# A new written-out order for a two-branch kernel, and D's second copies made with a maximum

## The chip, the core and the metric

The kernel runs on one core of one Trainium2 chip. Its time is the device time of one execution in microseconds (us); of the kernel before three runs gave a median of 131.97 us (131.25 to 135.03). Of one execution there is a profile, and all trace times below are microseconds from the start of its span. The engines are called PE (matrix multiply), DVE (vector), ACT (scalar), POOL (GpSimd) and SP (here only the queue that issues nearly all transfers).

## The reference

Two independent branches over 2048 tokens of 448 channels, in bf16, are joined along the channels.

```python
# branch A: attention of 16 heads of 28 over 8 earlier tokens, 2 apart
idx = pos[:, None] - 2 * arange(8)[None, :]           # masked where negative
logits = einsum("bhsd,bhswd->bhsw", q, k[idx]) * 28 ** -0.5
a = einsum("bhsw,bhswd->bhsd", softmax(logits), v[idx]) @ wo
# branch B: a diagonal complex state-space model of 448 states
h_t = Lam_bar * h_{t-1} + B_bar @ x_t                 # Lam_bar = exp(dt * Lam)
b = 2 * (h @ C^T).real + x * Dskip
out = concatenate([a, b], axis=-1)
```

## The kernel before

**Steps and the order.** Every small piece of work is a Python function marked as a step (`@op`). One long string, `ORDER`, lists all 700 steps with their arguments; the kernel emits them in that sequence. A number behind `@` gives the PSUM bank or the buffer slot that a step takes, and a trailing `.` or `=` says whether ACT or DVE does an eviction or a scaling. Each engine runs its own instructions strictly in the sequence of the string, and semaphores hold an instruction until what it needs is there. So the string fixes the order on all engines, the order of the transfers on SP's queue, the banks and the buffers at once.

**Branch A.** `XI`, `XA`, `XH` and `xi`, `xa`, `xh` bring the input into transposed form (`xT`) by PE and evictions for the first half, `TX` by DMA transposes for the second. `QS` and `QT` compute a 512-token piece of q or k (three matmuls over full rows, one over the last 64 rows), `qk` and `qh` evict it. `VM`, `VT`, `v` do the same for v. `P(u, r, ws)` on DVE (L387) multiplies q with four shifted k at once; there are 28 of them, 14 for each half `u` of the tokens, in seven buffer slots of `prt`. `E_` sums the products of a head on PE, `lt` on ACT scales the logits of one half, `TD` turns them by a DMA transpose (L417). `sma` (DVE: mask, maximum, subtract), `smb` (ACT: Exp), `smc` (DVE: sum, reciprocal, multiply) are the softmax of one half. `AL`, `al`, `ad`, `sp` build banded matrices of the weights through DRAM, in buffers that `pm`, `pk` and `pw` clear on POOL, `AV` multiplies them with v, and `W_` applies `wo`.

**Branch B.** Time is cut into four phases `j` of 512 steps, states into seven groups `g` of 64 complex ones. `LB` loads x, four DMA transposes `xt` (L720) turn it into `xbuf`, of 14 blocks of 128x128 each, and one, `BD` (L678), turns the input matrix into `BT`, 28 blocks. `BU` and `BH` (L736, L743) project x on a group; each reads 512 columns to which all four `xt` contribute. `BR` adds the rotated earlier phase, `z` evicts, `UP`, `y`, `sa`, `sb`, `sd`, `DN`, `dn` run the scan over the last phase. `sw`, `hp`, `hy`, `hz` then carry the scan's state back into the other phases: `hp` makes scaled copies in numbered buffers, `hy` adds two of them (L864), and the last step of a group, `hz` (L869), adds the result into `Z`. `C(j, ct)` (L883) is an output group of seven matmuls, one for each `g`; for `j` under 3 it reads `Z` after `hz`, for `j` of 3 it does not. `CH` (L907) is one such group in two halves. `c` and `ch` evict with D's share of x added, `oc` and `oh` store. `CS` copies the transposed C matrix, and `ca`, `cb`, `cs` scale it.

**D.** `LD` loads the vector Dskip, broadcast to 128 partitions, as columns 0 to 447 of the tile `dsk`. `dk` (L729, L730) makes a second copy of it in columns 448 to 895, in two parts, and `xd` multiplies x by the tile.

Of the kernel before, what the change touches and what calls it, by code (L numbers as in the profile page):

```python
# [29 lines left out]


ORDER = """
LR LX24 LX02 WU@0 LH0 LQ10 XI1@0 xi11. xi10= LQ11 LH1 LQ00 LX48 LQ01 PP@1 pcopy pa XI2@2 xi20= LY1 LY2 LY0 LV LB111
LB001 LB121 LB011 LB000 TX3 TX2 TX0 XI0@3 TX1 pb pd_ xi00. pe QT030@2 QT020@1 pc xi01. ty0@0 tf0 LB021 QT040@0
QS020 ty5@1 tf5 WX qk020. QS030 qk030. pf QS050@3 QS040 ts00 qk040. LB101 QS060@2 QS000@1 P021@0 P020@1 XH1@4 xh1=
XA11@5 xa11. XA10@6 xa10. QS010@7 QT001@5 pg QT000 QT021@4 QT050 QT010 qk050. QT051@0 P041@2 P040@3 QT060 qh000.
qh001. QT011@6 qk000. qk010. P000@4 ts05 LC QS021 QS061@3 P001@5 QS001 QS011 QS051 ts10 ts15 qk001. qk011. P011@6
qk051. ts25 qk021. VM110@7 QS031@1 VM100@6 ts20 VT110 QT061 ty2@1 tf2 QT031 qk031. VT100 v100. qh010. E_00@0 E_02
E_04 P030@2 VM101@4 xt3 qh011. VM001@6 v110. ts02 QS041@1 LN1 P010@3 VT101 v101. LB110 QT110@7 QT041 QT130@3
QT111@5 QT120@2 VT001 P031@0 qk041. P051@1 QS111 ts12 hc0 LN0 P060@5 ts22 qk111. ty1@1 tf1 v001. QS101@1 ty6@0  # L40
QS130 QS110 QS120 qk120. qk110. ts01 QS141@6 QS100@5 ci3. CD3 VM400@2 P050@4 E_01@7 E_03 E_05 qk130. ci2. CD2
QT151@3 VT400 QT100 qk100. tf6 ts06 P061@3 ts11 QT141 QT150@4 QT101 qk101. ts21 E_06 lt01 v400. qk141. QS150
VM511@5 QS151 QS131@1 LB120 qk151. P121@1 P101@5 P120@3 lt00 QS121@2 VT500@6 qk150. QT131 LB100 xt1 TD0 LB020
qk131. ty3@1 QT140@3 VT511 P110@4 QT160@7 QT121 qk121. VM500 QS140 v500. P100@0 v511. QS161@1 xt2 bx= QS160 qh100.
qh101. hc1 P151@2 E_10@6 E_12 P111@6 E_11@5 LB010 BD VT510@7 QT161 ts16 VT000@2 qk140. P131@0 P130@6 VM011@4 qh110.
xt0 VM000 v000. P141@4 VM510 v510. P150@1 VM501@3 VM410@2 VM411@7 ts26 qh111. VM010@1 ci1. P140@3 VT410 ty4@0 LD
CD1 VT501 v501. VT010 v010. P160@5 VT011 v011. ci0. E_13 E_15 E_14 VM401@1 P161@0 E_16 v410. VM111@4 lt10 ab lt11
VT411 BH32@6 VT401 sma0 smb0 v401. BH10@2 CD0 VT111 OZ TD1 rb0 tf4 BH00@5 BU10 BU00 v111. z00. v411. BU20@3 BU01@0
OP pw BU30@1 z10. wo BH30 BH01 dk smc0@0 CS BH51@5 BH20 z20. BH11@4 BH40@7 BR01 z01. z30. BU40 z40. sma1 BU11 BR11
rb3 z11. AL0@1 al0. AL1@7 al1. tf3 smb1 BU31@4 smc1@0 BH13@1 ca1= ca3= ts03 BH02@7 BH23@0 BH12@3 BH31 BH03@2 cb3=  # L50
xd0 BU02 BR02 z02. BR31 BU12 BR12 z12. BU13 BU03 BR03 cb4. z31. pm01 pm12 pm02 BR13 z03. z13. cb0. BU32 BR32 UP0
pm13 ts13 cb6= UP1 pm03 AX@4 z32. y1. AL2@3 pm11 pk pm21 pm10 AL3@7 pm00 pm22 y0. sa0 ca0= BU21@6 sb0 ca6= ad1 ax.
BH50@2 cb5= BH41@4 BH33@1 al2. ts04 BH22@3 ca2. BH21 BR21 BU33 BU22 ts14 ad0 z21. BR33 BR22 sp1 al3. ts24 z22. BU50
BU23 BR23 sd0 cb2= cb1= ca5. BU41 BR41 z33. ad2 ts23 DN1@3 dn1 z23. z50. UP3 y3= pm20 pm23 adx sp0 UP2 DN0@7 dn0
z41. y2. cs0 sa2 hp001@3. hp021. BU60@2 BU51 BR51 BH42@7 ca4= hp000@2. BH52@0 hp020. BH60 ad3 BH43@1 spx BH63@4
BH53@3 hp010. z51. BU42 z60. BR42 z42. BU52 AV010@5 AV000@6 sw0 sb2 av000. BR52 BU43 z52. cs2 BR43 hp011. av010.
BU53 BR53 z53. sd2 DN2@0 z43. DN3@6 cs4 dn2 AV031@7 av031. dn3 cs6 AV001@5 UP5 y5. hp101@4= UP4 hp100@0= hp110= y4.
sa4 AV030@0 av030. hp003@1. sp2 hp121= AV011@7 AV020@3 av020. AV021@6 sp3 BH62@1 BH61@0 BU61 BR61 av021. z61. BU62
W_00@6 BR62 BU63 sb4 av011. av001. W_31@5 hp120= z62. BR63 hp013. W_11@1 sd4 hp023. hy0 z63. hp002@6. UP6 DN5@7 dn5
y6. sa6 w31@0. sw2 hp012. hp022. W_30@0 DN4@4 dn4 sw4 w30@1. w11@2. w00@3. hp005@0. hp025. W_21@7 ow00 w21@4.  # L60
W_10@5 W_20@4 w20@5. hp015. sb6 W_01@1 hp111= sd6 C32@6 ow21 hz0 hy1 DN6@7 dn6 AV110@0 ow20 AV100@4 AV131@3 AV120@2
av110. AV130@7 hz1 ow30 hp103@7= hp102@5= AV101@0 hp123= av100. hp113= av120. hp112= hy3 hp105@3= hp122= av130.
hp104@2= hp114= hp125= AV111@4 av101. hz3 AV121@2 av121. av111. w10@3. av131. sw6 hy2 w01@5. hp004@7. hp124= W_60@7
w60@1. hp024. hp014. hz2 hy4 hp115. hy5 hp106@3= W_70@0 ow60 ow31 hp116. ow01 hz4 W_50@4 w50@1. W_41@5 hp006@2.
W_40@1 W_61@7 w61@5. ow11 hp126= hz5 w40@2. ow40 hp026. W_71@3 C30@2 C31@4 W_51@7 C33@1 hp016. hy6 hz6 w71@2= xd2
w70@0. w41@4. ow70 C10@0 c10@0 xd3 c30@1 oc30 xd1 c31@2 C02@5 C22@3 ow41 ow10 C13@0 c13@3 oc13 c33@1 oc33 c22@4
oc31 ow50 C03@2 c03@5 w51@3= c02@3 oc03 oc22 ow71 oc02 ow61 C11@4 C12@1 c11@1 ow51 C01@2 c01@2 oc01 oc11 c12@5 oc12
C21@4 c21@4 c32@3 C20@2 c20@6 oc32 oc21 C00@4 oc20 oc10 c00@1 CH0@2 ch0@5 CH1@6 oc00 ch1 oh0 oh1
"""

@with_exitstack
def kernel(
# [653 lines left out]

    @op
    def dk():
        V.tensor_copy(dsk[:, 512:896], dsk[:, 0:384])  # L729
        V.tensor_copy(dsk[:, D:512], dsk[:, 384:D])  # L730
# [273 lines left out]
```

## Time and profile before

| | before |
|---|---|
| median of three runs | 131.97 us |
| the profiled execution's own time | 131.99 us |
| its span in the trace | 130.3 us |
| PE busy | 119.8 us (92%) |
| DVE busy | 115.3 us (88%) |
| ACT busy | 99.3 us (76%) |
| POOL busy | 21.5 us (17%) |
| mean granted PE clock | 0.987 |
| moved by DMA | 23.02 MB, mean 177 GB/s |

Busy shares are means over the whole span: ACT has nothing to do in the last 18 us, when PE works through the output groups and DVE evicts them. A busy PE is one that has matmuls in its pipeline, at whatever clock. The idle time in front of an instruction is put down to what released it last.

### The profile page before, as it was taken

To read this page: it belongs to the slowest core of one execution; us is meant where nothing else is said; L and a number is where in the kernel's file an instruction comes from. 1 tells how busy PE (TensorE), PEld (TensorE's weight loads), DVE (VectorE), ACT (ScalarE), POOL (GpSimd) and SP (SyncE) were. 2 spreads that over 40 slices of the span, in tenths; PEclk is the share of its full clock that TensorE was granted. 3 is DMA by queue.
4 is the path that set the end of the run, shared out by engine and by line. 5 is a ranking of instruction groups with operands and counts; after the bars stand their busy time and mean duration, and the time that the engine had idled before them with its cause. 6 is when DMAs were issued, how large, how long until landed. Compare 5 with 4: busy or idle time off the path is not lost.

```text
span 130.3 us, 2886 instructions
## 1 busy us (share of the span) xinstructions
PE 119.8 (92%) x1046; PEld 57.8 (44%) x1046; DVE 115.3 (88%) x229; ACT 99.3 (76%) x204; POOL 21.5 (17%) x50
## 2 busy tenths in 40 slices
PE   6969999999999992899999999999999959999990
PEld 6525343343443430235354444555566424455560
DVE  5788999999999998499499999999999995999871
ACT  3479999999999999348999999999999949100000
POOL 6811300000000000699980000000000000000000
PEclk9999999999999999679999999999999999999999
DMA  3999998899999999996599895799863031115673
GB/s 96 265 245 301 310 149 172 248 247 205 119 276 223 185 211 149 198 240 166 225 264 122 268 167 190 142 135 144 142 171 101 34 107 35 35 35 166 226 240 113
DMA packets 55317, 23.02 MB, mean 177 GB/s; under 512 B 41127, under 2 KB 54503, under 8 KB 55303
## 3 DMA queue, kind: packets, MB, share of 16 engines
q1 hardware_dynamic: 55240, 22.84, 82.4%
q8 instruction: 8, 0.13, 0.5%
q14 instruction: 6, 0.05, 0.2%
q10 hardware_dynamic: 63, 0.01, 0.0%
HBM read 9.74 MB, written 6.37 MB: 124 GB/s over the span
## 4 chain that ended last, share of the span: by engine, by line
PE 43%; DVE 34%; DMA 8%; issue 6%; ACT 3%; SPq 2%; ACTq 1%; DVEq 0%
PE ps L883 13%; PE ps L351 13%; DVE pr L387 5%; DMA wq<-in_A_wqkv_dram 4%; PE ps L736 4%; DMA xbuf<-xnB 4%; DVE hs L791 3%; PE ps L515 3%; DVE p L777 2%; DVE p L776 2%; PE ps L357 2%; PE ps L399 2%; DVE Z L869 2%; ACT Z L125 2%; DVE Ak L864 2%
## 5 line engine op out<-in xcount | busy, mean ns | idle before, releaser
L387 DVE TENSOR_TENSOR pr<-qf,kf 128x2048 bf16<-128x2048 bf16 x24 | 27.8, 1219 | 0.7 <-ACT kf L125 0.6
L736 PE MATMUL ps<-xbuf,BT 128*128 128x512 bf16 x84 | 22.9, 404 | 0.0
L883 PE MATMUL ps<-Cw,Z 128*128 128x448 bf16 x105 | 20.7, 352 | 1.6 <-ACT ya L125 1.6
L351 PE MATMUL ps<-xT,wq 128*128 128x512 bf16 x84 | 19.8, 380 | 1.2 <-DMA wq<-in_A_wqkv_dram 1.2
L125 ACT CAST Z<-ps 128x512 bf16<-128x512 f32 (+1 forms) x34 | 15.9, 525 | 3.5 <-issue 2.2
L883 PEld LDWEIGHTS <-Z 128*128 128x128 bf16 x105 | 10.2, 98 | 11.6 <-issue 1.9
L553 PE MATMUL ps<-wo,oT 128*128 128x448 bf16 x64 | 13.3, 352 | 0.0
L736 PEld LDWEIGHTS <-BT 128*128 128x128 bf16 x84 | 8.2, 103 | 10.8 <-issue 3.8
L351 PEld LDWEIGHTS <-wq 128*128 128x128 bf16 x84 | 7.8, 98 | 11.8 <-DMA wq<-in_A_wqkv_dram 2.2
L948 POOL MEMSET PT<- 128x1080 f32 x12 | 11.5, 1006 | 0.0
L515 PE MATMUL ps<-wq,xT 128*128 128x448 bf16 x48 | 10.7, 353 | 0.0
L125 ACT CAST oT<-ps 128x512 bf16<-128x512 f32 x17 | 9.6, 651 | 0.2
L125 ACT CAST v_s<-ps 128x448 bf16<-128x448 f32 x16 | 8.3, 549 | 1.0 <-PE ps L522 0.8
L553 PEld LDWEIGHTS <-oT 128*128 128x128 bf16 x64 | 6.2, 98 | 5.8 <-issue 0.2
L857 ACT ACTIVATE Ak<-Z,acol 128x512 bf16<-128x512 bf16 x12 | 8.3, 744 | 0.0
L125 ACT CAST ya<-ps 128x448 bf16<-128x448 f32 (+1 forms) x15 | 8.0, 577 | 0.0
L743 PE MATMUL ps<-xbuf,BT 64*128 64x512 bf16 x28 | 5.1, 378 | 3.0 <-DMA xbuf<-xnB 3.0
L125 ACT CAST kf<-ps 128x512 bf16<-128x512 f32 x12 | 6.9, 603 | 0.8 <-PE ps L351 0.8
L750 PE MATMUL ps<-Z,R 128*128 128x512 bf16 x21 | 7.5, 381 | 0.0
L125 ACT CAST qf<-ps 128x512 bf16<-128x512 f32 x12 | 7.1, 593 | 0.4 <-PE ps L351 0.2
L515 PEld LDWEIGHTS <-xT 128*128 128x128 bf16 x48 | 4.3, 98 | 5.8 <-issue 2.2
L933 POOL MEMSET Z<- 128x14 bf16 x1 | 0.1, 112 | 38.6 <-PE ps L522 38.6
(177 smaller groups left out, 220.4 us busy)
## 6 DMA issues: line engine op xcount, KB each, us to landing
PT<-pd SPq DMA_DIRECT2D x16, 156.0 KB, 5.0
out_dram<-ya SPq DMA_DIRECT2D x16, 112.0 KB, 1.8
out_dram<-xbuf SPq DMA_DIRECT2D x15, 112.0 KB, 1.8
pd<-Ak SPq DMA_DIRECT2D x2, 640.0 KB, 4.1
xbuf<-in_A_x_dram SPq DMA_DIRECT2D x2, 448.0 KB, 6.1
xnB<-in_B_x_dram SPq DMA_DIRECT2D x4, 224.0 KB, 4.8
oT<-Cw SPq DMA_DIRECT2D x2, 392.0 KB, 4.9
xnB<-in_B_x_dram SPq DMA_DIRECT2D x4, 192.0 KB, 2.9
```

The costliest lines, as they stand in the source:

```text
L125: (ACT.copy if e == "A" else V.tensor_copy)(o, i)
L351: PE.matmul(p[:], wqk(m, slice(0, 128), kt), xT[:, u, 4 * s + kt], start=(first and kt == 0), stop=(not first and kt == 2))
L387: V.tensor_tensor(t, q.unsqueeze(1).to_broadcast((128, 4, 512)), k4, ALU.mult)
L515: PE.matmul(p[:, 0:D], xT[:, b0 // 4, 4 * s + kt, c + par:c + 256:2], wq[:, kt, 2 * D:3 * D], start=(first and kt == 0), stop=(not first a ...
L553: PE.matmul(p[:, 0:D], late["oT"][:, b // 4, hg, par, 128 * (b % 4):128 * (b % 4) + 128], late["wo"][:, hg, :], start=(hg == 0), stop=(hg ...
L736: PE.matmul(p[:], BT[:, g, f, :], xTB[:, j // 2, 4 * (j % 2) + f, :], start=(first and f == 0), stop=(not first and f == 2 and j == 0))
L743: PE.matmul(p[:], BT[r, g, 3, :], xTB[r, j // 2, 3, :], start=first, stop=(not first and j == 0))
L750: PE.matmul(pp["z", g, j][:], rot(g, 0), late["Z"][:, g, j - 1, :], start=False, stop=True)
L791: V.tensor_tensor_scan(hs[:, i], rk[:, 4, g0 + i:g0 + i + 1].to_broadcast((128, N2)), vv[:, i], 0.0, ALU.mult, ALU.add)
L857: ACT.activation(t, i, ACTF.Copy, scale=c)
L883: PE.matmul(p[:, 0:D], z, Cw[:, g, :], start=(g == 0), stop=(g == G - 1))
L948: POOL.memset(t.bitcast(F32), 0.0)
```

## The change

The string `ORDER` is written anew: the same 700 steps in another sequence, with other banks and buffer slots, and 18 evictions or scalings on the other of ACT and DVE. Apart from the string, `dk` makes its two copies as the maximum of the source with itself. All later lines move down by one.

```diff
 ORDER = """
-LR LX24 LX02 WU@0 LH0 LQ10 XI1@0 xi11. xi10= LQ11 LH1 LQ00 LX48 LQ01 PP@1 pcopy pa XI2@2 xi20= LY1 LY2 LY0 LV LB111
+LR LX24 LX02 WU@0 XI1@0 xi10. xi11= PP@1 pcopy pa pb pd_ XI2@2 XI0@3 xi01= LQ00 xi00. QS000@0 LX48 pe LQ01 LQ11 LH0
...
     @op
     def dk():
-        V.tensor_copy(dsk[:, 512:896], dsk[:, 0:384])
-        V.tensor_copy(dsk[:, D:512], dsk[:, 384:D])
+        for a, b, n in ((512, 0, 384), (D, 384, 64)):
+            V.tensor_tensor(dsk[:, a:a + n], dsk[:, b:b + n], dsk[:, b:b + n], ALU.max)
```

On SP's queue this is the piece around the DMA transposes, first as it stood. `xbuf<-xnB` is an `xt`, `attn<-lt` a `TD`, `BT<-Bn` is `BD`, `Cw<-Cn` turns the C matrix, and `xnB` and `Bn` from a DRAM tensor are loads.

```order
L683 DMA_TRANSPOSE Cw<-Cn 128x7x128
L252 DMA xnB<-in_B_x_dram 128x2x384
L252 DMA xnB<-in_B_x_dram 128x2x448
L720 DMA_TRANSPOSE xbuf<-xnB 128x14x128
L417 DMA_TRANSPOSE attn<-lt 128x8x128
L252 DMA xnB<-in_B_x_dram 128x2x384
L720 DMA_TRANSPOSE xbuf<-xnB 128x14x128
L252 DMA xnB<-in_B_x_dram 128x2x64
L678 DMA_TRANSPOSE BT<-Bn 128x28x128
L720 DMA_TRANSPOSE xbuf<-xnB 128x14x128
L725 DMA dsk<-in_B_Dskip_dram 128x448
L683 DMA_TRANSPOSE Cw<-Cn 128x7x128 x2
```

One `xt` stands still earlier on the queue, between the loads of C and of B. The same piece in the new order:

```order
L253 DMA xnB<-in_B_x_dram 128x2x64
L253 DMA xnB<-in_B_x_dram 128x2x384
L418 DMA_TRANSPOSE attn<-lt 128x8x128
L679 DMA_TRANSPOSE BT<-Bn 128x28x128
L721 DMA_TRANSPOSE xbuf<-xnB 128x14x128 x4
L726 DMA dsk<-in_B_Dskip_dram 128x448
L684 DMA_TRANSPOSE Cw<-Cn 128x7x128
L684 DMA_TRANSPOSE Cw<-Cn 128x7x64
L684 DMA_TRANSPOSE Cw<-Cn 128x7x128
L418 DMA_TRANSPOSE attn<-lt 128x8x128
```

All twelve loads of x now stand ahead; the first `TD`, `BD` and the four `xt` follow one another, and D's load comes behind them.

On DVE this is the piece around the first softmax, as it stood. `pr` are the products `P`, the rows with `attn` and `m` are `sma`, those with `zc` are `smc`, `R` is a rotation table, `kM` and `frt` are a step `tf`.

```order
L387 TENSOR_TENSOR pr<-qf,kf 128x2048 x7
L387 TENSOR_TENSOR pr<-qh_t,kh 128x2048 x2
L423 TENSOR_TENSOR attn<-attn,mk 128x256
L425 TENSOR_TENSOR m<-attn 128x512
L426 TENSOR_TENSOR m<-m 128x8x32
L427 TENSOR_TENSOR m<-m 128x8x16
L429 TENSOR_TENSOR attn<-attn,m 128x1024
L672 TENSOR_TENSOR R<-Is,co 128x7x128
L655 TENSOR_SCALAR kM<-iot,fT 128x256
L656 SCALAR_TENSOR_TENSOR frt<-kM,frt 128x256
L729 COPY dsk<-dsk 128x384
L730 COPY dsk<-dsk 128x64
```

And in the new order, from the end of `sma` on:

```order
L430 TENSOR_TENSOR attn<-attn,m 128x1024
L388 TENSOR_TENSOR pr<-qf,kf 128x2048 x5
L388 TENSOR_TENSOR pr<-qh_t,kh 128x2048 x2
L440 TENSOR_TENSOR zc<-attn 128x512
L441 TENSOR_TENSOR zc<-zc 128x8x32
L442 TENSOR_TENSOR zc<-zc 128x8x16
L443 RECIPROCAL zc<-zc 128x8x16
L444 TENSOR_TENSOR attn<-attn,zc 128x1024
L731 TENSOR_TENSOR dsk<-dsk 128x384
L731 TENSOR_TENSOR dsk<-dsk 128x64
L673 TENSOR_TENSOR R<-Is,co 128x7x128
L656 TENSOR_SCALAR kM<-iot,fT 128x256
```

Seven products moved from ahead of `sma` to behind it, where ACT's Exp of the first half runs, and `dk` moved behind `smc`.

More of the change, by code (lines that the diff above doesn't have):

```diff
@@ L32 @@
 ORDER = """
-LR LX24 LX02 WU@0 LH0 LQ10 XI1@0 xi11. xi10= LQ11 LH1 LQ00 LX48 LQ01 PP@1 pcopy pa XI2@2 xi20= LY1 LY2 LY0 LV LB111
[L34 to L67, printed above, removed]
@@ L68 @@
-C21@4 c21@4 c32@3 C20@2 c20@6 oc32 oc21 C00@4 oc20 oc10 c00@1 CH0@2 ch0@5 CH1@6 oc00 ch1 oh0 oh1
+LR LX24 LX02 WU@0 XI1@0 xi10. xi11= PP@1 pcopy pa pb pd_ XI2@2 XI0@3 xi01= LQ00 xi00. QS000@0 LX48 pe LQ01 LQ11 LH0
+pc XH1@3 XA10@1 LH1 ty0@0 LQ10 tf0 QS010@4 LY0 LY2 LY1 LN1 LV TX1 TX2 TX3 TX0 xh1= xi20= XA11@3 QS050@2 QS030@5 pf
+ty5@1 tf5 xa10. xa11. pg LC QT000 qk000. QT050 LN0 QT001@3 QT010 qk010. P000@0 QT031@1 QT020@6 QT011@7 ts05 QT030
+qk030. QS020 qk020. ts15 P001@1 P020@2 QS011 P021@3 ts00 LB111 ts10 QS001 qk001. ts20 WX QS060@6 QS031 LB100
@@ new lines @@
+QS021@5 qk050. VT100@3 QT051@4 QT021 QT060 qk011. P011@4 LB120 P010@5 LB011 ty2@0 tf2 qk031. LB121 LB001 QT040@2
+QT041@0 qk021. qh000. QS041 P030@6 QS051 qk051. LB000 LB020 LB110 ts25 ty1@1 tf1 qh001. QS040 qk041. VM100 ts02
+v100. VM001@4 VM101@5 QS061@1 ts01 E_01@6 E_00@0 qk040. E_02 QT061 qh010. VT001 QT150@2 QT110@3 ts12 QT111@7 LB101
+LB010 LB021 qh011. ts22 QS111 qk111. ts11 QS110 v001. qk110. QS150 QS101@1 QS140@7 QS120@4 ts21 P050@5 P031@3 hc0
+qk150. QT101 QT140 P051@2 ci2. qk101. VT111@3 bx. P040@1 E_03 E_05 P041@0 E_04 QT121@2 QT120 P060@4 ty6@1 qk120.
@@ new lines @@
+P061@3 VT101 QT130@1 E_06 lt00 tf6 QS130 P110@3 lt01 TD0 BD qk130. xt1 xt2 xt0 xt3 QS121 QS131@6 QS100@1 P111@4
+VT510@0 QT160@4 P120@0 ci3. QT131 qk140. P140@1 v101. qk121. QT141@7 QT100 qk100. LD VM111 ts06 QS160 qh100. QS141
+VM510 VM400@1 QS161@2 QS151@5 v111. qh101. VM110@4 VT110 QT151 QT161 hc1 ty3@0 VT400 v510. qk131. P100@2 ci1.
+P121@5 P101@6 E_10@6 E_12 E_11@0 sma0 qk141. qk151. P150@5 CD2 P151@4 ts16 v110. VT500@5 VT511@7 v400. qh111.
+VT410@3 VT501@4 ts26 qh110. CD3 VM511 v511. VM410 VM000@1 v410. VM011@2 VM501 v501. smb0 VM010@3 VM401@7 CD1
@@ new lines @@
+VM411@4 VM500 v500. P141@3 VT000 VT411 VT010 v000. P130@0 P131@6 E_13 E_14 E_15 ty4@1 VT401 VT011 BH00@1 P161@2
+v010. v401. P160@0 E_16 lt11 smc0@0 BU00 BH20@7 BH30@0 BH11@3 lt10 ci0. TD1 OZ CD0 OP ab BH10@5 dk v011. BH01@6
+BU20 pm22 pm01 rb0 z20. v411. BU10 z10. BU30 z30. AL0@4 al0. ad0 tf4 AL1@5 al1. z00. BU11 BR11 z11. BU01 BR01 z01.
+BU12@1 sma1 smb1 BH03@3 BH32@6 BH21@5 BH22@4 BH31@0 BH12 BH02@7 rb3 BH13@2 BU31 BU02 tf3 ts03 BR02 z02. smc1@0 BR31
+CS ca4= xd0 ca2= BR12 z12. BU03 BR03 ts13 z31. z03. ts04 BU13 BR13 z13. ca0. BU32 BR32 UP0 y0. UP1 y1. ca6= sa0
@@ new lines @@
+AX@0 ad1 ax. cb1= sb0 ca1= sd0 cb4= BU21 BR21 AL3@2 BU22 ts14 z21. cb6. pm03 z32. ca5. cb5= pw BU23@5 pm10 pm00
+pm02 sp0 adx ca3= BR22 BU33@6 BH40@0 pk BH33 BH23 BH41@3 z22. al3. pm12 pm21 pm23 cb3. ts24 BH42@4 pm13 pm11 BH50@1
+sp1 BH51@2 pm20 AL2@7 al2. BR23 cb2= ad3 BR33 wo ad2 z23. z33. BU40 z40. ts23 BU50 cb0= z50. UP3 DN0@7 UP2 y2. dn0
+DN1@0 dn1 hp000@3. BU41 BR41 cs2 cs6 cs0 y3. sa2 BU51 BR51 z41. hp020. z51. cs4 sb2 hp001@2= BU42 AV010@3 av010.
+sd2 AV000@6 av000. AV001@5 av001. sw0 AV021@0 AV030@2 AV031@1 AV020@3 AV011@7 sp3 spx sp2 BH52@6 BU52 BR42 av011.
@@ new lines @@
+BR52 av031. av021. hp101@1= hp111= hp121= hp100@0= z42. z52. BH43@1 BH61@7 BH53@0 BH60@5 hp011. av020. BU43 BR43
+z43. BU53 hp021. BR53 DN2@3 dn2 DN3@6 dn3 sw2 hp120= hy1 z53. UP4 y4. BU60 UP5 av030. y5. sa4 BH63@3 BH62@1 z60.
+hp002@4. hp012. hp110= W_00@6 w00@0. BU61 BR61 z61. sb4 hp010. hy0 BU62 W_01@5 w01@1. BR62 sd4 z62. hz1 W_20@7
+hp003@5. W_31@6 BU63 hp022. w31@2. BR63 z63. W_30@1 DN5@6 w20@3. DN4@5 ow01 dn5 hp023. UP6 y6. dn4 ow31 sw4 sa6
+AV121@0 AV130@7 AV111@2 hp102@6= sb6 hp122= sd6 AV100@6 hp112= av121. AV101@3 av111. AV120@5 W_21@0 AV110@2
@@ new lines @@
+hp103@7= av101. av120. hp113= hy2 av100. av110. av130. hp123= ow00 AV131@5 av131. hp013. hp004@9. w21@0. W_10@3
+W_70@2 hp024. W_51@7 W_11@5 w30@2. hp104@8= hp124= hy3 hp114= ow30 DN6@6 dn6 sw6 w51@1. ow20 W_40@4 w40@4. hp014.
+hp005@7. ow51 hz2 hp006@6. W_60@0 W_61@7 hp015. w61@2. w10@5. ow10 W_71@6 W_41@4 hp025. w71@3. hz0 hy4 hp105@4=
+hp115= hp125= C30@1 C33@7 hz4 C31@6 hp026. hp016. w70@5. hy5 ow71 C32@3 W_50@2 hp106@9= hp116. ow21 hz5 hz3 hp126.
+hy6 hz6 w41@0. ow41 w60@3. C00@4 C21@0 ow60 c00@0 xd2 w50@3= ow50 oc00 ow61 c30@1 ow70 oc30 xd3 c32@2 c33@3 oc33
@@ L69 @@
+C13@4 CH0@2 xd1 w11@5= c21@1 oc21 c13@3 C11@1 c11@0 C22@3 c22@4 c31@5 oc32 oc11 ow40 ow11 C12@7 c12@2 oc12 oc13
+oc22 oc31 C02@0 c02@1 ch0@0 oc02 C03@1 c03@6 C01@6 c01@7 oc01 oh0 C10@2 c10@4 C20@6 c20@7 oc03 oc10 oc20 CH1@2 ch1
+oh1
 """
```

## The prediction

> **What bounds the kernel now.** I read the page first, then the waits, then the timelines of PE, DVE, ACT and of SP's DMA queue.
>
> ```profile
> span 130.3 us, 2886 instructions
> PE 119.8 (92%) x1046; PEld 57.8 (44%) x1046; DVE 115.3 (88%) x229; ACT 99.3 (76%) x204; POOL 21.5 (17%) x50
> PEclk9999999999999999679999999999999999999999
> ```
>
> PE and DVE are both nearly full, so a new order can only win the few waits that are left, and can lose anywhere. The list of waits names them (total, times, longest):
>
> ```profile
> PE ps L743 <- DMA xbuf<-xnB: 3.0, 1, 3.0
> DVE dsk L729 <- DMA dsk<-in_B_Dskip_dram: 2.1, 1, 2.1
> DVE zc L439 <- ACT attn L433: 1.8, 1, 1.8
> PE ps L883 <- ACT ya L125: 1.6, 1, 1.6
> DVE Ak L864 <- ACT Ak L857: 1.5, 1, 1.5
> ```
>
> On PE's timeline (start, duration) the first of them costs more than its 3.0 us:
>
> ```profile
> 8.73 3.41 PE L351 MATMUL ps<-xT,wq 128*128 128x512 bf16 x15 [0.52 <-DMA wq<-in_A_wqkv_dram]
> 49.20 0.36 PE L522 MATMUL ps<-wq,xT 64*128 64x448 bf16 x1
> 52.53 0.37 PE L743 MATMUL ps<-xbuf,BT 64*128 64x512 bf16 x1 [2.97 <-DMA xbuf<-xnB]
> 53.27 5.10 PE L736 MATMUL ps<-xbuf,BT 128*128 128x512 bf16 x15
> 107.67 1.48 PE L883 MATMUL ps<-Cw,Z 128*128 128x448 bf16 x7 [1.63 <-ACT ya L125]
> 109.75 16.23 PE L883 MATMUL ps<-Cw,Z 128*128 128x448 bf16 x84
> 125.81 1.50 PE L907 MATMUL ps<-Cw,Z 128*128 128x224 bf16 x14
> ```
>
> Behind the wait 15 matmuls of 512 columns take 5.10 us where 15 like them took 3.41: the clock was down (the 6 and 7 of the page's row), another 1.7 us. PE's removable loss is 2.97 + 1.7 + 1.63 = 6.3 us.
>
> DVE decides the end. Every output group C(j, ct) with j under 3 reads all of Z, which is complete with the last `hz` (L869), and 12 groups' worth (11 of `C`, two halves in `CH`) stand behind it.
>
> ```profile
> 12.67 0.43 DVE L125 COPY xT<-ps 64x512 bf16<-64x512 bf16 x1
> 30.49 1.22 DVE L387 TENSOR_TENSOR pr<-qh_t,kh 128x2048 bf16<-128x2048 bf16 x1
> 53.78 0.55 DVE L729 COPY dsk<-dsk 128x384 bf16<-128x384 bf16 x1 [2.12 <-DMA dsk<-in_B_Dskip_dram]
> 54.25 1.05 DVE L730 COPY dsk<-dsk 128x64 bf16<-128x64 bf16 x1
> 54.33 0.97 DVE L439 TENSOR_TENSOR zc<-attn 128x512 f32<-128x512 bf16 x1
> 63.54 0.69 DVE L439 TENSOR_TENSOR zc<-attn 128x512 f32<-128x512 bf16 x1 [1.81 <-ACT attn L433]
> 110.36 0.96 DVE L864 TENSOR_TENSOR Ak<-Ak,BT 128x1536 bf16<-128x1536 bf16 x1 [1.53 <-ACT Ak L857]
> 111.36 0.96 DVE L869 TENSOR_TENSOR Z<-Z,Ak 128x1536 bf16<-128x1536 bf16 x1
> ```
>
> The last `hz` ends at 111.36 + 0.96 = 112.32, and the span runs 130.3 - 112.32 = 17.98 us longer. DVE's own removable loss ahead of it is 2.12 + 1.81 + 1.53 = 5.46 us.
>
> **The change, part by part.** *Work.* The instructions of a step stay what they were but for `dk`. Eighteen evictions or scalings change between ACT and DVE; of those ahead of the last `hz`, seven come to DVE and seven leave it, none over 0.5 us, so DVE's sum there moves by about nothing, bounds -0.5 and +0.5. PE's work is the same.
>
> *dk.* The two copies hold DVE from 53.78, and the instruction behind them ends at 54.33 + 0.97 = 55.30 where its twin takes 0.69: without `dk` it would have ended at 54.47, so the pair costs 0.83. For two-input operations of 384 and 64 columns the nearest rows are the 512 and 128 columns of the softmax's maximum:
>
> ```profile
> 58.27 0.42 DVE L425 TENSOR_TENSOR m<-attn 128x512 bf16<-128x512 bf16 x1
> 59.05 0.22 DVE L427 TENSOR_TENSOR m<-m 128x128 bf16<-128x128 bf16 x1
> 53.38 0.84 POOL L948 MEMSET wo<- 128x896 f32 x1
> 54.16 5.84 POOL L948 MEMSET PT<- 128x1080 f32 x6
> ```
>
> They are pipelined, so about 0.4 for both: a gain of 0.4, bounds 0 and 0.8. POOL's memsets ran beside both copies, and they will run beside the maxima. A rule speaks against the edit: the Trainium skill ("VectorE: DVE Perf Modes", "The perf-mode tier table") gives a bf16 copy four elements a cycle and `tensor_tensor` two. By it and that page's 58 cycles at 0.96 GHz an estimate is 0.24 us for the copies and 0.35 for the maxima: a loss of 0.1, and a total 0.5 above mine; the 0.55 and 1.05 of the trace do not agree with the 0.24.
>
> *Transposes on SP's queue, and what starts them.* SP's rows (start, time to issue):
>
> ```profile
> 14.37 6.33 SPq L256 DMA_TRANSPOSE xT<-xbuf  x4
> 38.07 1.26 SPq L417 DMA_TRANSPOSE attn<-lt  x1
> 42.99 4.19 SPq L678 DMA_TRANSPOSE BT<-Bn  x1
> 47.27 1.61 SPq L720 DMA_TRANSPOSE xbuf<-xnB  x1
> 48.93 1.19 SPq L725 DMA_DIRECT2D dsk<-in_B_Dskip_dram  x1
> 52.83 1.44 SPq L417 DMA_TRANSPOSE attn<-lt  x1
> ```
>
> Before, three of the four `xt` stand early, between loads, and the last behind `BD`; every `BU` needs all four. Now all loads come first, then TD0, BD and four `xt` in one row: 8 + 28 + 56 = 92 blocks of 128x128. The row starts when TD0's wait ends: after E_06, which needs P061. P061 is the 14th product in both orders and ended at 31.71; one `tf` (0.87) less and one small copy (0.3) more stand ahead, so 31.1. E_06 and the two `lt` behind it take 0.6 + 0.5 + 0.5, so TD0 issues at about 32.9 instead of 38.07. Price of a block: the last `xt` alone is 1.61/14 = 0.115, BD 4.19/28 = 0.15, and BD with the `xt` behind it, from 42.99 to their user's start at 52.53, 9.54/42 = 0.23 with start and landing in it; the four `xT` were issued at 6.33/28 = 0.23. I take 0.15 a block and, from 47.27 + 1.61 to 52.53, 3.6 us of landing and stalls once: 32.9 + 13.8 + 3.6 = 50.3. Bounds 47.1 (0.115) and 54.1 (0.23, landing included).
>
> *PE.* It was through with all work ahead of the first `BH` at 49.20 + 0.36 = 49.56. The same work stands ahead now. New is that E_06 comes when P061 is only just done: PE reaches it about 0.7 us early and waits. So PE asks for `xbuf` at about 50.3, as it lands: a wait near 0, bounds 0 and 3.8. Both the 2.97 and the clock's 1.7 go.
>
> *D and the second softmax.* The rows for these are from DVE, from ACT and from ACT's waits:
>
> ```profile
> 37.50 8.11 DVE L387 TENSOR_TENSOR pr<-qf,kf 128x2048 bf16<-128x2048 bf16 x7
> 62.43 1.08 ACT L433 ACTIVATE attn<-attn 128x1024 bf16<-128x1024 bf16 x1
> 108.98 1.35 ACT L857 ACTIVATE Ak<-Z,acol 128x512 bf16<-128x512 bf16 x2
> ACT Z L125 <- issue: 2.2, 1, 2.2
> ACT BT L857 <- DVE Ak L864: 1.6, 1, 1.6
> ACT Z L125 <- PE ps L743: 1.4, 1, 1.4
> ```
>
> DVE runs on from P061's 31.1: a `tf` (0.87), fourteen products of 1.14 (8.11 for seven, overlapped) and `sma0` (2.0) bring `smc0` to 49.9, and its 3.7 bring `dk` to 53.6. D's load follows the row of transposes at 46.7 and lands by 51.5 if it again takes up to the 53.78 - 48.93 = 4.85 it took: the 2.12 goes, and comes back if the row is over 2 us late. Five small steps (5.4) then bring `smc1` to 59.4. `smb1`, the Exp that it needs, waits on ACT for `z01`; PE comes there some 6 us after 50.3, Exp ends at about 56.8 + 0.5 + 1.08 = 58.4. The 1.81 goes, margin 1.0.
>
> *The last `hp`.* ACT's `hp116` waited for a buffer that DVE's `hy5` had to free (the 1.6), and `hy6` then for ACT, done at 108.98 + 1.35 = 110.33. The buffers are dealt anew (slots 8 and 9 are new), so I take that 1.6 off with the 2.2 and 1.4 of the starved middle: 105.1. DVE comes to `hy6` at 106.5 - 1.9 = 104.6 by the sum below: the 1.53 goes, and about 0.6 comes back, bounds 0 and 1.5.
>
> *Sum.* Last `hz`: 112.32 - 5.46 - 0.4 = 106.5. PE reaches its first dependent group at 109.75 + 1.32 (one group of seven, 16.23/84 x 7 = 1.35) - 6.3 + 0.7 = 105.5, just ahead. The span would be 106.5 + 17.98 = 124.5. To this I add new waits of DVE: second softmax's transpose (TD1 waits for E_16; 0.3, bounds 0 and 1.3), the landing of `CS` ahead of `ca` (0.3, 0 to 1.4), the last `hp` (0.6, 0 to 1.5), small waits where margins are near 0 (0.5, bounds 0 and 2, one to four like the 0.52 of PE's first row): 1.7 in all, bounds 0 and 6.2. Span 126.2. The profiled execution took 131.99 for a span of 130.3; 1.7 more than the span gives 127.9. The median of the runs shown is 131.97, so no correction.
>
> **Order of the head.** LQ00 now stands ahead of LX48, LH0 and LQ10 behind. First real matmuls: before at 8.73 steadily. Now QS000 waits for xi01 on DVE (about 7.4), then the weights come in the order of their use; I count no gain, bounds -0.6 and +1.
>
> **Rivals.** *A, the row of transposes is late (slower).* It is the longest unbroken row of transposes on the queue, with nothing to put between. By 0.23 a block and one landing of 3.6 added, it ends at 32.9 + 21.2 + 3.6 = 57.7; PE waits 57.7 - 50.3 = 7.4 us at the first `BH`, the clock falls as at 52.53 (1.7), ACT's Exp and `dk` follow. PE's first dependent group would come at 105.5 + 7.4 + 1.7 = 114.6 against 111.1 (109.75 + 1.35) before: 3.5 us later, 135.5. It decides from a landing of about 56.5 on, which makes 134.3. For it: 6.33/28 at the head. Against: BD's 4.19/28 and the last `xt`.
>
> *B, the gain is eaten.* The row lands at 54.1: PE waits 3.8 and loses 1.7 of clock, `dk` waits again, and only the two late waits go: 1.63 + 0.8 of the 6.3 stay won, less some of the 1.7 of new waits: about 131. Or ACT becomes the bound. For it: ACT is as full as the other two in the late middle (columns: window, length, then each engine's busy time).
>
> ```profile
> 90.00:104.50 14.50, 14.45 (x224) 8.46 (x223) 14.30 (x34) 14.50 (x30) 0.00 (x0) 1.00 0.54 117
> ```
>
> Against: the starved middle took 3.6 us from ACT alone.
>
> *C, the plan holds throughout.* No new waits: 124.5 + 1.7 = 126.2; with the low bounds of the rest, 125.7.
>
> **How the numbers follow.** Forecast (waits of about 1.7, within 1.2 of 127.9): 0.46. C: 0.16. B (129.2 to 134): 0.24. A: 0.14. Time: 127.9. Range 125.7 to 132.6: its low end is C's, its high end goes through B. The likeliest case alone is 126.7 to 129.1. Measurement tells about 2% (2.6 us) from no change: faster below 129.3, slower above 134.6. Faster takes the forecast, C and a little of B: 0.66. Within 2%: most of B and a little of A, 0.21. Slower: 0.13.
>
> **What would show it.** Right: no wait of L744 for `xbuf<-xnB` over 1 us, PEclk without the 6 and 7, TD0 issued near 33, the last `hz` (L870) ending near 108, about 18 us from there to the end, `dsk` rows under 0.3 us each with no wait for its DMA, waits of `zc` and of the last `hy` under 0.5. Wrong: PE idle over 3 us at the first `BH`; the last `hz` after 111; or PE later than DVE at the first group that needs Z.

## The result and the profile after

The changed kernel takes 143.31 us (median of 4 runs, 142.53 to 143.9) against 131.88 for the kernel before on the same chip: a ratio of 1.088, with a 95% interval of 1.080 to 1.096. Forecast were 127.9 us. The profiled execution took 143.09 us for a span of 141.4. Medians here and below are over all runs of a kernel, but a ratio compares only runs in the faster of two states in which the same kernel can run, so that it can differ a little from the quotient of the medians.

These are the head of the page and one of its groups (busy time, mean ns of one, idle before), then two rows of the list of waits:

```profile
span 141.4 us, 2879 instructions
PE 122.1 (86%) x1036; PEld 59.2 (42%) x1046; DVE 125.0 (88%) x229; ACT 99.9 (71%) x204; POOL 21.0 (15%) x50
PEclk9999999999999999999655999999999999999999
L656 DVE TENSOR_SCALAR kM<-iot,fT 128x256 f32<-128x256 f32 x7 | 13.4, 1919 | 0.0
ACT attn L434 <- DVE attn L430: 10.7, 1, 10.7
PE ps L751 <- ACT Z L126: 10.4, 1, 10.4
```

The wait for `xbuf` that stood first on PE's list is gone, and a new one of 10.4 us has come. Followed back, PE waits for ACT, ACT waits for DVE, and DVE waits for nothing: it is *busier* by 9.7 us than before (125.0 against 115.3). A group of seven small instructions holds 13.4 us at a mean of 1919 ns, though its members took 0.35 each. A mean so far from the usual asks for the rows one by one. DVE's timeline (start, duration):

```profile
52.94 0.68 DVE L440 TENSOR_TENSOR zc<-attn 128x512 f32<-128x512 bf16 x1
...
56.57 0.45 DVE L731 TENSOR_TENSOR dsk<-dsk 128x384 bf16<-128x384 bf16 x2
...
57.95 11.37 DVE L656 TENSOR_SCALAR kM<-iot,fT 128x256 f32<-128x256 f32 x1
...
72.40 0.34 DVE L656 TENSOR_SCALAR kM<-iot,fT 128x256 f32<-128x256 f32 x1
...
73.12 0.69 DVE L440 TENSOR_TENSOR zc<-attn 128x512 f32<-128x512 bf16 x1
```

One instruction, the `kM` of `tf4`, shows as busy for 11.37 us; its twin at 72.40 takes 0.34. It ends at 69.32. On POOL's timeline something ends at that time:

```profile
53.49 0.72 POOL L819 TENSOR_SCALAR acol<-co 64x21 f32<-64x21 f32 x2
54.29 0.61 POOL L819 TENSOR_SCALAR bcol<-co 64x21 f32<-64x21 f32 x2
54.84 2.86 POOL L949 MEMSET PT<- 128x1080 f32 x3
...
62.36 1.16 POOL L949 MEMSET ya<- 128x1280 f32 x1
63.47 5.70 POOL L949 MEMSET PT<- 128x1080 f32 x6
```

POOL clears its buffers in one row without a break, up to 63.47 + 5.70 = 69.17. So the trace suggests, but doesn't show, that the row held the `kM`. Against it stood a row of the kernel before: there `tf3`'s `kM` ran amid the same memsets in 0.35.

```profile
59.95 1.16 POOL L948 MEMSET oT<- 128x1280 f32 x1
60.92 0.35 DVE L655 TENSOR_SCALAR kM<-iot,fT 128x256 f32<-128x256 f32 x1
61.05 1.32 POOL L948 MEMSET ya<- 128x1280 f32 x1
```

Read closely, that row also shows a dispute: the memset that starts at 61.05 took 1.32 where its like takes 1.16, so POOL gave way once. What differs between the two kernels is what POOL does ahead of the row: the change moved `ab` (four small `tensor_scalar`s) from the head to the place right in front of it.

### The profile page after: what moved, and what is told of

Read it like the earlier page. It is cut to its first block, busy times and chain, and to the rows that moved or that the text cites. A ratio compares the mean times of both kernels' runs of the same rounds, so it can differ in the third digit from the quotient of the medians.

```text
span 141.4 us, 2879 instructions
## 1 busy us (share of the span) xinstructions
PE 122.1 (86%) x1036; PEld 59.2 (42%) x1046; DVE 125.0 (88%) x229; ACT 99.9 (71%) x204; POOL 21.0 (15%) x50
## 4 chain that ended last, share of the span: by engine, by line
PE 57%; DVE 26%; DMA 7%; issue 4%; ACT 3%; SPq 1%; DVEq 0%
PE ps L352 14%; DVE kM L656 8%; PE ps L516 7%; PE ps L554 6%; PE ps L737 6%; PE ps L884 5%; PE ps L400 3%; DMA PT<-Z 3%; PE ps L358 3%; DMA out_dram<-ya 2%; PE ps L541 2%; PE ps L523 2%; PE ps L751 2%; PE ps L219 2%; DVE xbuf L891 2%
## 5 line engine op out<-in xcount | busy, mean ns | idle before, releaser
L352 PE MATMUL ps<-xT,wq 128*128 128x512 bf16 x80 | 21.1, 403 | 2.2 <-ACT xT L126 1.7
L737 PE MATMUL ps<-xbuf,BT 128*128 128x512 bf16 x79 | 22.2, 398 | 0.5 <-issue 0.3
L126 ACT CAST Z<-ps 128x512 bf16<-128x512 f32 (+1 forms) x35 | 17.2, 536 | 1.1 <-PE ps L763 0.6
L751 PE MATMUL ps<-Z,R 128*128 128x512 bf16 x20 | 7.4, 402 | 10.4 <-ACT Z L126 10.4
L352 PEld LDWEIGHTS <-wq 128*128 128x128 bf16 x84 | 8.3, 103 | 12.6 <-issue 5.2
L656 DVE TENSOR_SCALAR kM<-iot,fT 128x256 f32<-128x256 f32 x7 | 13.4, 1919 | 0.0
L554 PE MATMUL ps<-wo,oT 128*128 128x448 bf16 x64 | 13.4, 353 | 0.0
L949 POOL MEMSET PT<- 128x1080 f32 x12 | 11.4, 994 | 0.0
L516 PE MATMUL ps<-wq,xT 128*128 128x448 bf16 x48 | 10.1, 353 | 0.0
L434 ACT ACTIVATE attn<-attn 128x1024 bf16<-128x1024 bf16 x2 | 2.1, 1056 | 10.7 <-DVE attn L430 10.7
```

Of the source, the lines that this page charges most:

```text
L126: (ACT.copy if e == "A" else V.tensor_copy)(o, i)
L352: PE.matmul(p[:], wqk(m, slice(0, 128), kt), xT[:, u, 4 * s + kt], start=(first and kt == 0), stop=(not first and kt == 2))
L516: PE.matmul(p[:, 0:D], xT[:, b0 // 4, 4 * s + kt, c + par:c + 256:2], wq[:, kt, 2 * D:3 * D], start=(first and kt == 0), stop=(not first a ...
L554: PE.matmul(p[:, 0:D], late["oT"][:, b // 4, hg, par, 128 * (b % 4):128 * (b % 4) + 128], late["wo"][:, hg, :], start=(hg == 0), stop=(hg ...
L656: V.tensor_scalar(kM, iot[:], fT[:, g:g + 1], MAGIC, ALU.mult, ALU.add)
L737: PE.matmul(p[:], BT[:, g, f, :], xTB[:, j // 2, 4 * (j % 2) + f, :], start=(first and f == 0), stop=(not first and f == 2 and j == 0))
```

## Experiments: what held DVE

"Before" is 131.9 us in the first four runs, 131.8 in the next eight and 132.0 in the last three.

**e1_ab_early.** One step moved in the order, on POOL alone (pieces of longer lines):

```diff
-xa10. xa11. pg LC
+xa10. xa11. pg ab LC
-OZ CD0 OP ab BH10@5 dk
+OZ CD0 OP BH10@5 dk
```

> The changed kernel with one step moved on POOL alone: ab (four small tensor_scalars on halves of the partitions, which ran at 53.49 to 54.90, right ahead of the row of memsets) stands behind pg in the head. Theory ROW (a tensor_scalar of DVE that is issued inside POOL's unbroken row of memsets waits for the end of the row): the row starts and ends some 1.3 us earlier, tf4's kM still takes about 10 us, total about 142. Theory STEP (POOL's parts are put out of step by ab's half-partition instructions, so that they never reach the gap between two memsets together; without ab ahead DVE gets in at the next gap, as tf3 and the copies did in the kernel before): kM takes 1.4 us or less, total 131 to 133. Theory ELSE (POOL has nothing to do with it): kM 11.4, total 143.

Measured: 133.14 us, ratio 1.011 (1.005 to 1.017); 10.2 of the 11.4 us are gone. POOL and DVE there:

```profile
54.15 2.88 POOL L949 MEMSET PT<- 128x1080 f32 x3 [0.43 <-PE ps L404]
57.76 3.02 POOL L949 MEMSET PT<- 128x1080 f32 x3
58.14 1.70 DVE L656 TENSOR_SCALAR kM<-iot,fT 128x256 f32<-128x256 f32 x1
62.94 1.14 DVE L656 TENSOR_SCALAR kM<-iot,fT 128x256 f32<-128x256 f32 x1
68.09 0.81 DVE L699 TENSOR_SCALAR oT<-oT,c2t 128x448 bf16<-128x448 bf16 x1
```

The same memsets stand beside the same instructions, and three `tensor_scalar`s of DVE now get in between two memsets after 0.5 to 1.4 us instead of at the row's end. One thing differs besides `ab`: POOL now stands idle for 0.43 us ahead of the row. ROW and ELSE fall. STEP's total holds (131 to 133 forecast) and its bound on `kM` nearly (1.4, against 1.70); its reason isn't shown by this.

**e3_before_ab_late.** The reverse, in the kernel before: `ab` behind `OP`.

> The kernel before with ab moved behind OP on POOL, so that it stands right ahead of the row of memsets, as in the changed kernel. STEP: the first copy of dk, a two-port form issued at about 53.8, waits for the end of the row near 69.5 instead of 0.4 us, and the total is 142 to 147. ROW in a weaker form (DVE gets in by chance of the moment): dk takes up to 2 us as before, total within 1.5 us of 132. ELSE: 132.

Measured: 138.72 us, ratio 1.046 (1.037 to 1.055). The copies of `dk` came while `ab` itself ran and took 0.26 and 0.17; the victim was another, `tf3`'s `kM`:

```profile
63.27 5.69 POOL L948 MEMSET PT<- 128x1080 f32 x6
60.77 8.33 DVE L655 TENSOR_SCALAR kM<-iot,fT 128x256 f32<-128x256 f32 x1
```

It ends at 69.10, with the row (68.96). I had the wrong instruction, and so the wrong size; the effect can be put into the old kernel by moving `ab` alone.

**e4_two_inputs.** Nothing moved, another form of the same arithmetic:

```diff
-V.tensor_scalar(kM, iot[:], fT[:, g:g + 1], MAGIC, ALU.mult, ALU.add)
+V.scalar_tensor_tensor(kM, iot[:], fT[:, g:g + 1], cols[:, 5:6].to_broadcast((128, N2)), ALU.mult, ALU.add)
```

> The changed kernel with nothing moved, but kM made as scalar_tensor_tensor with the constant as a second input from SBUF, in all seven tf. If it is the form of the instruction that POOL's memsets hold up (ROW and STEP): kM about 0.43 in its old place, total 131.5 to 133.5. ELSE, or if two inputs from SBUF are held up too: kM about 11, total 143.

Measured: 133.47 us, ratio 1.014 (1.008 to 1.020).

```profile
57.23 0.48 DVE L656 SCALAR_TENSOR_TENSOR kM<-iot,fT,cols 128x256 f32<-128x256 f32 x1
62.76 5.69 POOL L949 MEMSET PT<- 128x1080 f32 x6
65.44 3.15 DVE L699 TENSOR_SCALAR oT<-oT,c2t 128x448 bf16<-128x448 bf16 x1
```

With `ab` in its late place, the two-input form passes in 0.48; the next `tensor_scalar` in line, `ca4`, is now the one that waits until the row's end (68.45). So the hold depends on the form of DVE's instruction and on what POOL did ahead of the row together.

**e2_tf_early.** `tf4` and `tf3` behind `ty4`, ahead of the memsets.

> The changed kernel with tf4 and tf3 moved ahead of POOL's memsets on DVE, behind ty4, near 50 us. ROW and STEP alike: both kM take 0.35, nothing of DVE's is held during the memsets, total 131 to 133 (143.3 less the 11.0 of the wait, with up to 1 us either way for what follows). ELSE: the wait comes back at another instruction, total over 140.

Measured: 136.69 us, ratio 1.037 (1.030 to 1.044). Both `kM` took 0.35 and no other `tensor_scalar` was held by more than 0.4, but the new place had a price of its own. In the profiled execution, of 138.13 us:

```profile
52.94 0.43 DVE L657 SCALAR_TENSOR_TENSOR frt<-kM,frt 128x256 f32<-128x256 f32 x1 [2.41 <-ACT frt L650]
66.56 0.69 DVE L440 TENSOR_TENSOR zc<-attn 128x512 f32<-128x512 bf16 x1 [2.29 <-ACT attn L434]
```

ACT reaches `ty4` only 2.4 us after DVE asks for it, and the second softmax then waits 2.3 for its Exp. I had moved a consumer without looking at its producer.

**e5_half and e6_full.** `ab` early as in e1, and other work in its old place: four memsets on halves of the partitions, or four `tensor_scalar`s on all of them, into a tile nobody reads.

```diff
+for h in (0, 64, 64, 0):                      # e5
+    POOL.memset(junk[h:h + 64], 0.0)
+for r in (0, 1, 1, 0):                        # e6
+    POOL.tensor_scalar(junk[:], co[:, 0:T - 1, r], 1.0, None, ALU.mult)
```

> ab early as in e1, and in its old place on POOL four memsets of an unused 21-column tile, on partitions 0 to 63, 64 to 127, 64 to 127 and 0 to 63 in ab's order. If it is instructions on half of the partitions that put POOL's parts out of step: tf4's kM waits for the end of the row of memsets again, about 11 us, total about 143. If it is something else in ab (its reads, its tensor_scalars): kM under 2 us as in e1, total about 133.

> ab early as in e1, and in its old place on POOL four tensor_scalars of 21 columns on all 128 partitions into an unused tile. If half partitions are the cause: kM under 2 us, total about 133. If a tensor_scalar ahead of the row is the cause whatever its partitions: kM about 11, total about 143.

Measured, one run each: 137.84 and 142.54 us. POOL's work ahead of the row and the `kM`s, first of e5, then of e6:

```profile
52.42 0.61 POOL L824 MEMSET junk<- 64x21 f32 x4
56.90 2.70 DVE L656 TENSOR_SCALAR kM<-iot,fT 128x256 f32<-128x256 f32 x1
62.70 4.90 DVE L656 TENSOR_SCALAR kM<-iot,fT 128x256 f32<-128x256 f32 x1
```

```profile
52.22 1.42 POOL L824 TENSOR_SCALAR junk<-co 128x21 f32<-128x21 f32 x4
56.68 11.37 DVE L656 TENSOR_SCALAR kM<-iot,fT 128x256 f32<-128x256 f32 x1
```

Full partitions hold DVE just as long (11.37), so STEP's reason, parts of POOL out of step through half-partition instructions, is refuted. Plain memsets ahead of the row also hold, but less: 2.70 and 4.90 lie between the two cases that I had expected of e5.

**e14_gap and e15_one.** The changed kernel with an idle stretch between `ab` and the row; and e1 with one `tensor_scalar` in the old place instead of four.

```diff
+ACT.copy(junk[:, 0, 0:1], hpib)               # e14: POOL waits for this
+POOL.memset(junk[:, 0], 0.0)
+POOL.tensor_scalar(junk[:], co[:, 0:T - 1, 0], 1.0, None, ALU.mult)   # e15
```

> The changed kernel with ab in its place, but with one more short memset of POOL between ab and the row that waits for a small copy by ACT behind v011: the row starts at about 56.5 instead of 54.84, after POOL stood idle for 1 us or more. If it is the unbroken succession of ab and the row that keeps DVE out: tf4's kM under 2 us, total 133 to 135. If what ab does to POOL outlasts an idle stretch: kM 12 to 13 us, total near 145.

> ab early as in e1 and one tensor_scalar of 21 columns on all partitions in its old place on POOL, where e6 had four. If one instruction that reads SBUF right ahead of the row is enough: kM about 11, total 142 to 143. If it takes the length of four (1.4 us): kM under 3, total 133 to 135.

Measured, one run each: 133.83 and 131.86 us. Again POOL ahead of the row and the first `kM`, of e14, then of e15:

```profile
56.63 0.10 POOL L824 MEMSET junk<- 128x7 f32 x1 [1.59 <-ACT junk L823]
56.72 3.02 POOL L954 MEMSET PT<- 128x1080 f32 x3
58.09 0.71 DVE L656 TENSOR_SCALAR kM<-iot,fT 128x256 f32<-128x256 f32 x1
```

```profile
52.36 0.27 POOL L823 TENSOR_SCALAR junk<-co 128x21 f32<-128x21 f32 x1
52.82 2.87 POOL L953 MEMSET PT<- 128x1080 f32 x3 [0.20 <-PE ps L404]
56.81 0.75 DVE L656 TENSOR_SCALAR kM<-iot,fT 128x256 f32<-128x256 f32 x1
```

With `ab` where the change put it, 1.59 us of idle POOL end the hold: 9.5 us come back. So `ab` alone isn't enough; it takes `ab`, or e6's four instructions, and the row without a break. In e15 POOL stood idle too, for 0.20 us, because one instruction is so short that the row's first memset still had to wait for PE; so e15 doesn't tell one instruction from four.

## Experiments: where the rest went

e1 still is 5.2 us over the forecast. Its traces differ from the prediction in two more places: the tail behind the last `hz`, and the middle, which comes late. I took the head for the cause of the second.

**e9_tail.** In the changed kernel and in e1 the span runs 19.4 to 19.6 us past the last `hz`, against 17.98 before. In e1 these rows stand there:

```profile
111.14 0.96 DVE L870 TENSOR_TENSOR Z<-Z,xbuf 128x1536 bf16<-128x1536 bf16 x1
119.76 0.62 DVE L126 CAST ya<-ps 128x448 bf16<-128x448 f32 x1 [1.26 <-DMA out_dram<-ya]
126.67 0.56 DVE L893 TENSOR_TENSOR xbuf<-ps,xnB 128x384 bf16<-128x384 f32 x1 [0.90 <-DMA out_dram<-xbuf]
128.19 0.63 DVE L891 TENSOR_TENSOR xbuf<-ps,xnB 128x448 bf16<-128x448 f32 x1 [0.84 <-DMA out_dram<-xbuf]
```

The new numbering deals output tiles to slots whose last tile is still being stored. The edit gives each tile of C its own slot (pieces; the other numbers in the order and the slot of `CH` are changed to fit):

```diff
-yo = pp["yo", j, ct] = xnA[:, slot()]
+yo = pp["yo", j, ct] = xnA[:, slot() + (4 if j < 3 else 0)]
-w11@5=
+w11@1=
```

> e1 with the output tiles of C on 16 slots instead of 8, this time with the slots above 9 made by an offset in c (j = 3 on slots 0 to 3, the others from 4 on), and w11 in slot 1 of ya. If the waits for stores (1.3, 0.9 and 0.8 us on DVE in e1) are the tail's loss: none of them over 0.2, 17.8 to 18.4 us past the last hz against 19.6 in e1, total 131.4 to 132.2. If the tail is held elsewhere: 133.1 as e1.

Measured: 131.28 us, ratio to before 0.992 (0.988 to 0.997).

```profile
110.99 0.96 DVE L870 TENSOR_TENSOR Z<-Z,xbuf 128x1536 bf16<-128x1536 bf16 x1
```

No wait for a store is left. The last `hz` ends at 110.99 + 0.96 = 111.95 and the span is 129.9: 17.95 past it, the old tail.

**e7_tail** was the first try, and a miss of mine:

> e1 with every output tile of C in a slot of its own in xbuf (16 slots for 16 tiles instead of 8), and w11 in slot 1 of ya, free for long, instead of 5. In e1 DVE waits 1.3, 0.9 and 0.8 us for the stores of the tiles that held those slots, and the span runs 19.6 us past the last hz, against 17.98 in the kernel before. If these waits are the tail's loss: 17.8 to 18.3 us past the last hz, total 131.2 to 132.0 against e1's 133.1. If PE's groups of seven matmuls set the tail anyway: 133.1.

Measured: 138.16 us. The order's numbers are read digit by digit, so slots 10 to 15 all became slot 1: six tiles shared one slot, `ch0` wrote over the tile of `c02` before its store (so the output is wrong), and DVE waited 2.86, 2.24 and 2.80 us for stores. It measured the opposite of what it was made for, and in that it agrees: of these 7.9 us most go into the tail, which runs 137.2 - 112.36 = 24.8 us past the last `hz`, 6.9 more than in e9.

**e8_head.** e1 with another head (pieces of longer lines):

```diff
-pa pb pd_ XI2@2 XI0@3 xi01= LQ00 xi00. QS000@0
+pa XI0@3 xi01= XI2@2 LQ00 xi00. xi20= pb pd_ QS000@0
+QS010@4 QT000 qk000. QT010 qk010. xh1= P000@0 P001@1 XA10@1
```

> e1 with the head's order mended on DVE, ACT and PE: xi01 and xi20 stand ahead of pb and pd_ on DVE, and QT000, QT010 with their evictions and P000, P001 stand right behind QS010. In the changed kernel the first product waits for kf until 15.83, where the kernel before had two products done by 12.63. If the head is what makes the middle late: the first product starts at 12 to 13.5, smc0 at 50 to 51 instead of 53.1, total 130.3 to 131.8. If the middle is held by P061 and the row of transposes whatever the head does: smc0 stays at 52.5 to 53, total about 133.

Measured: 134.93 us, slower than e1. The first two products came at 11.55, but I had put `XA10` behind them, and its eviction behind ACT's table load:

```profile
15.31 0.80 PE L358 MATMUL ps<-xT,wq 64*128 64x512 bf16 x5 [2.36 <-ACT xT L126]
```

`smc0` came at 55.15, 2.0 us later than e1's 53.14, and the end 1.8 later: this delay went through to the end nearly whole.

**e10_head, e11_all, e13_all_wx.** e10 keeps `XA10` early; e11 adds e9's slots and e4's form for `tf3` and `tf4`; e13 is e11 with `ab` behind `WX`.

> e1 with the head's order mended as in e8, but XA10 and XA11 stay early on PE and xa10, xa11 ahead of pf's table load on ACT (in e8 PE waited 2.4 us for xa10, and the whole middle came 2.0 us later for it). If the head is what makes the middle late: first product near 11.5 and no wait of PE over 0.5 us behind it, smc0 at 50.3 to 51.3 instead of 53.1, total 130.3 to 131.5. If P061 and the row of transposes hold the middle anyway: smc0 at 52.5 to 53.2, total 132.5 to 133.3.

> e1 with the heads of e10, the slots of e9, and kM of tf3 and tf4 alone made with the second input from SBUF, as in e4. By the sum of the three: head 2.0, tail 1.5, and 1.0 to 1.9 of waits for a gap between memsets: 128.2 to 129.5, faster than the kernel before. If they hide one another: 130 to 131.5.

> e11 with ab one place later on POOL, behind WX, so that WX (the copy of the weights of the seventh row group) no longer waits behind ab for DVE's pg (POOL's copy ran at 16.06 in e11, 11.91 in the changed kernel, and PE waited 1.9 us for it). If that wait is why e10's head gave 0.9 us at smc0 instead of 2 to 2.7: the products run without a gap from 17.3 on or earlier, smc0 at 50.3 to 51.3 instead of 52.2, total 129.5 to 131.0. If something else holds the middle: smc0 stays at 52, total 131.3 to 132.

Measured: 132.87 us (ratio 1.008, 1.004 to 1.012), 131.75 (0.997, 0.993 to 1.001) and 131.39 (0.989, 0.983 to 0.995). `smc0` comes at 52.18, 52.20 and 51.69 against e1's 53.14. That looks like a gain of 1.0 to 1.5 us, but the profiles of other runs forbid the reading. Here is `smc0` of e6, whose head is the change's own, and then of e13:

```profile
51.67 0.68 DVE L440 TENSOR_TENSOR zc<-attn 128x512 f32<-128x512 bf16 x1
```

```profile
51.69 0.68 DVE L440 TENSOR_TENSOR zc<-attn 128x512 f32<-128x512 bf16 x1
```

In the nine traces with the change's head and the same order of DVE ahead of `smc0` (the changed kernel, e1, e4 to e7, e9, e14 and e15) the first product starts anywhere from 14.58 to 16.02, and `smc0` from 51.67 to 53.14. Of the four kernels with another head only e8 lies outside that. So neither the new heads nor `ab` behind `WX` are shown to be worth anything at `smc0`. Nor are they at the end: e10 doesn't differ from e1 (132.87 and 133.14), nor e11 from e9 (131.75 and 131.28), and the intervals of e9's and e13's ratios overlap. The sum of the parts that I expected of e11, 128.2 to 129.5, did not come. What is clear of noise is e9: with the hold and the slots mended, the change's order is worth 0.8% by its ratio.

**e12_before_dk.** The kernel before with the maxima in `dk` and nothing else:

> The kernel before with nothing changed but dk: maxima of D with itself instead of the two copies. The prediction's price: dk and the instruction behind it take 0.4 us less, because maxima don't wait for POOL's memsets. If that reaches the end: 131.4 to 131.6. If DVE's later wait for the second Exp (1.8 us) takes it back: 131.8 to 132.0. If the copies are cheaper, as their rate would have it: 132.0 to 132.2.

Measured: 131.67 us, ratio 0.999 (0.995 to 1.003).

```profile
54.48 0.46 DVE L730 TENSOR_TENSOR dsk<-dsk 128x384 bf16<-128x384 bf16 x2 [2.24 <-DMA dsk<-in_B_Dskip_dram]
54.86 0.69 DVE L439 TENSOR_TENSOR zc<-attn 128x512 f32<-128x512 bf16 x1
...
61.15 1.27 DVE L655 TENSOR_SCALAR kM<-iot,fT 128x256 f32<-128x256 f32 x1
```

From the start of `dk` to the end of the row behind it: 54.86 + 0.69 - 54.48 = 1.07, against 1.52 with the copies. The 0.45 is there, and `tf3`'s `kM`, which fell between two memsets before, now waits 0.9 for one. Nothing measurable reaches the end. The gain is not a cheaper operation but the memsets that the maxima don't wait for: in e3, where the copies met `ab` and no memset, the same stretch is 54.48 + 0.70 - 54.22 = 0.96, 0.11 less than with the maxima. That is the loss of 0.1 which the prediction worked out for its rival.

## Why the prediction was wrong, point by point

**The step that failed** is *Work*: "The instructions of a step stay what they were", so that a `tf` costs its 0.87 wherever it stands and "DVE's sum there moves by about nothing, bounds -0.5 and +0.5". Beside POOL's row the `tf` cost 11.8, and DVE's busy time grew by 9.7. In the prediction's terms, the "Five small steps (5.4)" between `dk` and `smc1` took 73.12 - 57.02 = 16.1 us; in e1, with `ab` away from the row, 64.46 - 57.22 = 7.2. The prediction had the row in view, but asked of it only whether it disturbs `dk` ("POOL's memsets ran beside both copies, and they will run beside the maxima"). Two signs in the profile of before were passed over: the copy of 64 columns took 1.05 us, which it ended just when a memset ended, and `tf4` stood at 50.78, ahead of the row, while the new order puts it behind `dk`. That `ab` moved to the row's front was in the order of POOL, which the prediction didn't read. The Trainium skill ("SBUF — State Buffer", "Who interferes with whom") says that `copy`, `cast` and `tensor_scalar` can take the port pair that DVE shares with POOL, that the later of the two then blocks entirely, and that a `tensor_tensor` with both inputs in SBUF collides only with POOL's reads. The runs agree: the maxima (0.45) and the two-input form (0.48) pass, `tensor_scalar`s wait. By that rule the `kM` would have waited for the end of one memset, at most 1.16 us; the trace has the rest of one and eleven more, and the measurement decides.

**The size.** `ab`'s place: 143.31 - 133.14 = 10.2 us. The tail's slots: 133.14 - 131.28 = 1.9 (by the traces, 19.6 - 17.95 = 1.65). What is left of the change is a gain of 0.8% by e9's ratio, about 1 us, where 4.1 us were forecast.

**dk.** Price right (0.4 forecast, 0.45 shown by e12), effect on the time none. D's load was no longer waited for, as forecast.

**The row of transposes.** PE's rows and SP's:

```profile
35.64 1.74 SPq L418 DMA_TRANSPOSE attn<-lt  x1
37.42 4.32 SPq L679 DMA_TRANSPOSE BT<-Bn  x1
41.86 8.08 SPq L721 DMA_TRANSPOSE xbuf<-xnB  x4
52.76 0.39 PE L744 MATMUL ps<-xbuf,BT 64*128 64x512 bf16 x1
```

92 blocks took 49.94 - 35.64 = 14.3 us to issue, 0.155 a block (0.15 taken); PE doesn't wait for `xbuf`, and its clock doesn't fall there. Rival A is out. All of it comes 2.7 us late: TD0 at 35.64, not 32.9 (the prediction's own terms, 31.1 + 0.6 + 0.5 + 0.5, make 32.7).

**The late middle** is the second term that was mis-sized. `smc0` stands at 52.94, not 49.9. The prediction counted the steps behind P061, but took P061's own end from the old trace (31.1, where DVE ended it at 33.6; 32.3 to 33.8 in the nine traces). The head is the suspect: "I count no gain, bounds -0.6 and +1" was said of it, and the first product starts at 15.83 where two were done by 12.63 before. But the runs don't show it. In e13 the first product starts at 11.10, and P061 still ends at 32.35. So of the 1.8 to 3.2 us by which `smc0` is late, the cause stays open.

**The tail** was taken as 17.98 "longer" in any order. Slots were part of the change and were looked at for `hp` alone; it is 17.95 only with slots free (e9).

**New waits.** 1.7 were added for others. Of these, in e1 the last `hy` waited 0.35 (0.6 forecast) and the one before it 0.39; the second softmax and `ca` waited 0. The waits for the second Exp (1.81) and for `hp` (1.53, of which the 0.35 came back) went as forecast. In e1 the held `tensor_scalar`s (1.35, 0.8 and 0.5 over their usual) took their place.

**PE's clock.** Behind the 10.4 us of waiting PE's granted clock was at 0.6 to 0.5 for three slices. That cost nothing at the end: the last `hz` moved by 121.99 - 112.10 = 9.9 us between the change and e1, and the hold itself by 11.37 - 1.70 = 9.7. So it is DVE that sets the end there.

The outcome lay outside every rival, since none of them had POOL in it.
